# Normalising row tile 0 on GpSimd, and summing half of the layernorm scale on VectorE

## The chip, the cores and the metric

The kernel runs on one core of one Trainium2 chip. The metric is the device time of one execution in microseconds. Most executions of the kernel before agree within 0.3%; each comparison below is made with runs of the kernel before on the same chip in the same rounds. All runs compared here are of the state "fast". Kernels of different rounds ran partly on different chips and are set side by side by their medians (the kernel before had 831.05 to 831.30 us there).

Engine names in the profile: PE is TensorE (products), PEld its weight loads, DVE is VectorE, ACT is ScalarE, POOL is GpSimd, SP is the engine whose queue issues the DMAs.

## The reference

One transformer block with adaptive layernorm: linear attention, then a gated feed-forward part. Only the first layernorm and the first product matter here.

```python
mod = (silu(c) @ w_mod).reshape(c.shape[0], 6, 1, -1)      # c: 1 x 1024, w_mod: 1024 x 6144
sa, ca, ga, sb, cb, gb = (mod[:, i] for i in range(6))
h = layernorm(x) * (1 + ca) + sa                           # x: 2048 x 1024
x = x + ga * linear_attention(h, wqkv, wo)                 # starts with h @ wqkv
...                                                        # feed-forward part: not touched
```

`sa` is the shift and `ca` the scale of the first layernorm. Each is a vector of 1024, the product of `silu(c)` with a 1024 x 1024 block of `w_mod`.

## The kernel before

A helper records every operation with what it reads and writes, and sets the semaphores from that; so every instruction carries the same source line, L176, and is told apart by its tiles. PSUM dependencies are kept by whole banks.

The first chunk of 512 rows has four row tiles of 128. They are normalised (`XRES`), transposed on TensorE, scaled, and used as the moving operand of the q products (a k-tile is 128 of the 1024 values over which these products sum). The scale comes from 64 one-column products per 1024 columns (8 column tiles x 8 k-tiles), into single columns of PSUM bank 0:

```python
def ln1_xn(st):                                    # normalise row tile st on VectorE
    P.dve("tensor_scalar", out=XRES[:, st, :], in0=XRES[:, st, :],
          scalar1=MV[:, st, 0:1], scalar2=RSTD[:, st:st + 1], op0=ALU.subtract, op1=ALU.mult)

def mod_sc(w, c0, ms):                             # scale or shift, column tiles ms, on TensorE
    for m in ms:
        for kt in range(NDT):
            P.pe("matmul", out=PS[:, 0, c0 + m:c0 + m + 1], lhsT=w[:, kt, m * 128:(m + 1) * 128],
                 rhs=SILUC[:, kt:kt + 1], start=mod_first[0], stop=(kt == NDT - 1), skip_group_check=True)
            mod_first[0] = False
```

The start and the first q products (`q_part` is one 128x128 by 128x512 product for each k-tile given):

```python
ca_load(0); wq_load(0, 2); ca_load(1); wq_load(2, 2); wq_load(4, 2); sa_load(1)   # ca_load: 512 columns
...
ln1_xn(0); tile_transposes(0)
ln1_xn_act(1); tile_transposes(1)                  # tile 1 is normalised on ScalarE
...
ln1_xn(2); ln1_xn(3)
mod_sc(WCA, 8, range(2)); fin_ca(0, 2)             # scale columns 0-255, then + 1 into MODCOL
tile_transposes(2, 3)
h0_first(0, "dve"); h0_first(1, "dve")             # scale k-tiles 0, 1
...
for nt in range(4):
    q_part(nt, qb[nt], (0,))
mod_sc(WCA, 8, range(2, 4)); fin_ca(2, 2)          # columns 256-511
... 10 more q products ...
mod_sc(WCA, 8, range(4, 8)); fin_ca(4, 4)          # columns 512-1023: 32 one-column products
for dt in (4, 5):
    h0_scale_only(dt)
for nt in range(7):
    q_part(nt, qb[nt], (2, 3))
act_stats(4)
for nt in range(7):
    if nt == 4:
        mod_sc(WSA, 0, range(6, 8)); fin_sa(6, 2)  # shift
        for dt in (6, 7):
            h0_scale(dt)
    q_part(nt, qb[nt], (4, 5))
...
```

Of the kernel before, what the change touches and what calls it, by code (L numbers as in the profile page):

```python
# [6 lines left out]
BF16 = mybir.dt.bfloat16  # L7
U8 = mybir.dt.uint8
ACT = mybir.ActivationFunctionType
# [253 lines left out]
def bass_adaLN_cond__linear_attn_block__swiglu_ffn__prompt_kernel(  # L263
# [22 lines left out]
    with ExitStack() as es:  # L286
# [6 lines left out]
        def T(name, off, shape, dt):  # L293
            n = 1
            for s_ in shape[1:]:
                n *= s_
            assert off % 32 == 0 and off + n * mybir.dt.size(dt) <= ARENA, (name, off, shape)
            return nc.alloc_sbuf_tensor_at(name, shape, dt, offset=base + off)
# [29 lines left out]
        ZCOL = T("zcol", SM + 2304, [128, NHG], FP32)  # L328
        RED = T("red", SM + 2336, [128, NDT], FP32)
        MASK4 = T("mask4", SM + 2368, [128, 4], BF16)  # L330
        BIASQ = T("biasq", SM + 2784, [128, NDT], FP32)
        SUMXH = T("sumxh", SM + 2816, [128, NST, 2], FP32)
        NMR = T("nmr", SM + 2944, [128, NST], FP32)
# [64 lines left out]
        for st in range(4):  # L398
            P.dma("x0_%d" % st, XRES[:, st, :], xv[:, st, :])

        def ca_load(p):
            P.dma("wca%d" % p, WCA[:, :, 512 * p:512 * p + 512], wmv[:, :, D + 512 * p:D + 512 * p + 512])

        def sa_load(p):
            P.dma("wsa%d" % p, WSA[:, :, 512 * p:512 * p + 512], wmv[:, :, 512 * p:512 * p + 512])
# [1 line left out]
        def wq_load(i, n=1):  # L407
            P.dma("wq%d" % i, WQK[:, i:i + n, 0:D], wqkvv[:, i:i + n, 0:D])

        ca_load(0)  # L410
        wq_load(0, 2)
        ca_load(1)
        wq_load(2, 2)
        wq_load(4, 2)
        sa_load(1)
# [27 lines left out]
        P.dve("memset", ap=MASK[:], constant=0.0)  # L443
        for h in range(4):
            P.dve("memset", ap=MASK[32 * h:32 * h + 32, 32 * h:32 * h + 32], constant=1.0)
        P.dve("memset", ap=MASK4[:], constant=0.0)
        for h in range(4):
            P.dve("memset", ap=MASK4[32 * h:32 * h + 32, h:h + 1], constant=1.0)
# [4 lines left out]
        def warm(n=1, bank=2):  # L453
            for _ in range(n):
                P.pe("matmul", out=PS[:, bank, :], lhsT=IDENT[:], rhs=E1[:, 0, :], start=True, stop=True)
# [61 lines left out]
                P.dve("tensor_copy", out=MODTMP[:, m:m + n], in_=PS[:, 0, m:m + n])  # L517
            P.dve("tensor_copy", out=MODCOL[:, 1, m:m + n], in_=PS[:, 0, m:m + n])

        def h0_scale_only(dt):  # L520
            P.dve("tensor_scalar", out=HT[:, 0, dt, :], in0=HT[:, 1, dt, :], scalar1=MODCOL[:, 0, dt:dt + 1],
                  scalar2=None, op0=ALU.mult)

# [27 lines left out]
            else:  # L551
                P.dve("tensor_copy", out=dst, in_=src)

        def h0_scale(dt):
            P.dve("tensor_scalar", out=HT[:, 0, dt, :], in0=HT[:, 1, dt, :], scalar1=MODCOL[:, 0, dt:dt + 1],
                  scalar2=MODCOL[:, 1, dt:dt + 1], op0=ALU.mult, op1=ALU.add)

# [16 lines left out]
        def act_stats(st, c0=0, mid=None):  # L574
            n = (D - c0) // 512
            junk0 = HT[:, 1, 0:2, :] if st < 8 else JUNK1
            for fn_, sc_, acc_ in ((ACT.Identity, 1.0 / D, SUMX), (ACT.Square, D ** -0.5, SUMSQ)):
                P.act("activation", out=junk0[:, 0:n, :], in_=XRES[:, st, c0:D].rearrange("p (a b) -> p a b", a=n),
                      func=fn_, scale=sc_, accum_out=acc_[:, st:st + 1])
                if mid is not None:  # L580
                    mid()
                    mid = None

        def act_mv_ops(st):
            return [
                lambda: P.dve("tensor_copy", out=MV[:, st, 0:1], in_=SUMX[:, st:st + 1]),
                lambda: P.dve("scalar_tensor_tensor", out=MV[:, st, 1:2], in0=SUMX[:, st:st + 1],
                              scalar=SUMX[:, st:st + 1], in1=SUMSQ[:, st:st + 1], op0=ALU.mult, op1=ALU.subtract),
            ]
# [3 lines left out]
                  op1=ALU.add)  # L593
            P.pool("tensor_tensor", out=RSTD[:, st:st + 1], in0=VE[:, st:st + 1], in1=NEGHALF[:, 0:1], op=ALU.pow)

        act_stats(2)
        s0_, s1_, s3_ = ln1_stats_ops(0), ln1_stats_ops(1), ln1_stats_ops(3)
        m2 = act_mv_ops(2)

        def tile_transposes(*js):  # L600
            for dt in range(NDT):
# [3 lines left out]
                         identity=IDENT[:])  # L605

        warm(13, bank=3)
        s0_[0]()
        s0_[1]()
        s1_[0]()  # L610
        s0_[2]()
        ln1_rstd1(0)
        s1_[1]()
        s1_[2]()
        ln1_rstd1(1)
        ln1_xn(0)
        tile_transposes(0)
        warm(5, bank=3)
        s3_[0]()
        ln1_xn_act(1)  # L620
        tile_transposes(1)
        warm(0, bank=3)
        m2[1]()
        m2[0]()
        neg_rstd(2)
        s3_[1]()
        s3_[2]()
        ln1_rstd1(3)
        ln1_xn(2)
        ln1_xn(3)  # L630
        mod_sc(WCA, 8, range(2))
        fin_ca(0, 2)
        tile_transposes(2, 3)
        h0_first(0, "dve")
        h0_first(1, "dve")
        raw_copy(4, "dve")
# [95 lines left out]

        def q_phase_chunk0(side):
            qb = [1, 2, 3, 4, 6, 7, 5]
            for nt in range(4):
                q_part(nt, qb[nt], (0,))
            mod_sc(WCA, 8, range(2, 4))
            fin_ca(2, 2)
            for dt in (2, 3):
                h0_first(dt, "dve")  # L740
            for nts, dts in (((4, 5), (0,)), (range(6), (1,)), ((6,), (0, 1))):
                for nt in nts:
                    q_part(nt, qb[nt], dts)
            mod_sc(WCA, 8, range(4, 8))
            fin_ca(4, 4)
            for dt in (4, 5):
                h0_scale_only(dt)
            for nt in range(7):
                q_part(nt, qb[nt], (2, 3))
            act_stats(4)  # L750
            for nt in range(7):
                if nt == 4:
                    mod_sc(WSA, 0, range(6, 8))
                    fin_sa(6, 2)
                    for dt in (6, 7):
                        h0_scale(dt)
                q_part(nt, qb[nt], (4, 5))
            mod_sc(WSA, 0, range(4, 6))
            fin_sa(4, 2, True)
# [437 lines left out]
```

## Time and profile before

| | before |
|---|---|
| time, median of 3 (range) | 831.13 us (830.97 to 832.21) |
| share of the chain of waits on TensorE | 98% |
| first q product | 12.29 us |
| TensorE idle after that | under 0.1 us at any place |
| two scalings of k-tiles 0 and 1 (VectorE) before it | 0.88 us |

The page's part on the chain that ended last, by engine, for the kernel before:

```profile
PE 98%; DMA 1%; DVE 0%; ACT 0%; SPq 0%; POOL 0%; issue 0%
```

The same chain in order of time; the columns are start in us, length in us, and what the chain stood on:

```profile
9.78 0.79 POOL rstd L176
...
10.60 0.56 DVE xres L176
...
11.20 1.01 PE ps L176 x15
...
12.29 814.80 PE ps L176 x4016
```

The chain goes through the last reciprocal root on GpSimd, the normalisation of the last tile on VectorE and 15 transposes; then it is TensorE without a break to the end. Whatever the first q product waits for sets the time one for one; after it, so does every product added or taken away and every wait of TensorE.

The timeline of the kernel before on TensorE; columns are start, length, engine, line, operation, tiles written and read, shapes, count, and in brackets the idle before it with what ended it:

```profile
12.29 1.02 PE L176 MATMUL ps<-ht,wqk 128*128 128x512 bf16 x4
13.15 0.54 PE L176 MATMUL ps<-siluc,wca 128*128 128x1 bf16 x16
13.56 2.32 PE L176 MATMUL ps<-ht,wqk 128*128 128x512 bf16 x10
15.71 0.94 PE L176 MATMUL ps<-siluc,wca 128*128 128x1 bf16 x32
16.51 4.91 PE L176 MATMUL ps<-ht,wqk 128*128 128x512 bf16 x22
```

From starts alone: 32 one-column products occupy 16.51 - 15.71 = 0.80 us, so 0.025 us each, and 10 q products 15.71 - 13.56 = 2.15 us, so 0.215 us each. (A product's own length, 0.38 us, overlaps the next and is of no use here.)

Two more groups matter for estimating what the change adds. First the running sum that the kernel already makes later for other rows of `w_mod` (count, then shortest, median and longest in ns, first and last start, shape):

```profile
L176 DVE SCALAR_TENSOR_TENSOR acc<-stg,siluf,acc x14: 1275/1278/1286, 84.3 to 125.6; 128x1024 f32<-128x1024 bf16 x14
...
L176 DVE TENSOR_TENSOR mhl<-acc,mhl x4: 1224/1226/1226, 99.6 to 279.2; 128x1024 bf16<-128x1024 f32 x4
```

And the scaling that GpSimd does in it:

```profile
L176 POOL TENSOR_SCALAR h2t<-h2t,modcol x32: 762/768/1180, 230.9 to 649.4; 128x512 bf16<-128x512 bf16 x32
```

### The profile page before, as it was taken

The page shows a single profiled execution, that of the slowest core. Times are in us where ns is not written, and L with a number is a line of the kernel's source. Part 1 is how long each engine was busy: PE and PEld are TensorE (multiplying, and loading weights), DVE is VectorE, ACT ScalarE, POOL GpSimd, SP SyncE. Part 2 cuts the span into 40 slices and gives each one's busy share as a digit, 9 for nine tenths or more (in the row PEclk, how much of TensorE's full clock was granted, in tenths as well). Part 3 has the DMA queues.
Part 4 walks back from the last instruction along what each step waited for, and adds up shares of the span by engine and source line. Part 5 has one row for each costly group of instructions (what it writes and reads, how often), then busy time and mean ns, then how long its engine had stood idle before and what let it go on. Part 6 is the DMA issues. An engine that isn't in the chain of part 4 may idle for free.

```text
span 829.3 us, 10017 instructions
## 1 busy us (share of the span) xinstructions
PE 823.3 (99%) x4083; PEld 378.8 (46%) x4083; DVE 312.9 (38%) x666; ACT 196.3 (24%) x335; POOL 40.5 (5%) x58
## 2 busy tenths in 40 slices
PE   8999999999999999999999999999999999999998
PEld 4544444454444444444444444444444444444444
DVE  5797986756955521121221111122111211221111
ACT  3658641323232111111111111111110111111011
POOL 1010000000130000030000003000000300000000
DMA  9969655938297986700455571045557004553000
GB/s 320 284 152 229 150 162 172 197 107 304 57 256 226 262 256 184 194 25 13 123 152 153 152 188 34 13 124 154 152 153 193 27 13 124 151 154 91 0 26 26
DMA packets 199246, 119.29 MB, mean 144 GB/s; under 512 B 57880, under 2 KB 182944, under 8 KB 199200
## 3 DMA queue, kind: packets, MB, share of 16 engines
q1 hardware_dynamic: 199184, 118.65, 53.0%
q8 instruction: 32, 0.52, 0.3%
q14 instruction: 14, 0.11, 0.0%
q10 hardware_dynamic: 16, 0.00, 0.0%
HBM read 100.67 MB, written 4.33 MB: 127 GB/s over the span
## 4 chain that ended last, share of the span: by engine, by line
PE 98%; DMA 1%; DVE 0%; ACT 0%; SPq 0%; POOL 0%; issue 0%
PE ps L176 98%; DMA xres<-in_A_x_dram 1%; ACT ht L176 0%; DVE xres L176 0%; SPq L176 0%; POOL rstd L176 0%; DVE stats L176 0%; DVE mv L176 0%; DVE ve L176 0%
## 5 line engine op out<-in xcount | busy, mean ns | idle before, releaser
L176 PE MATMUL ps<-h2t,gug 128*128 128x512 bf16 x896 | 211.7, 379 | 0.0
L176 PE MATMUL ps<-h2t,guu 128*128 128x512 bf16 x896 | 211.7, 379 | 0.0
L176 DVE TENSOR_TENSOR at<-sg,ps 128x512 bf16<-128x512 bf16 x112 | 77.0, 687 | 282.8 <-PE ps L176 281.2
L176 ACT ACTIVATE sg<-ps 128x512 bf16<-128x512 f32 x112 | 66.9, 597 | 309.7 <-PE ps L176 309.7
L176 PEld LDWEIGHTS ps<-h2t,guu 128*128 128x128 bf16 x896 | 87.7, 98 | 105.7
L176 PEld LDWEIGHTS ps<-h2t,gug 128*128 128x128 bf16 x896 | 87.6, 98 | 105.5
L176 PE MATMUL ps<-wd_a,at 128*128 128x512 bf16 (+1 forms) x512 | 112.4, 377 | 0.0
L176 PE MATMUL ps<-ht,wqk 128*128 128x512 bf16 x512 | 111.8, 379 | 0.1
L176 PE MATMUL ps<-wd_b,at 128*128 128x512 bf16 (+1 forms) x384 | 85.0, 377 | 0.0
L176 PEld LDWEIGHTS ps<-wd_a,at 128*128 128x128 bf16 x512 | 50.1, 98 | 59.7
L176 DVE TENSOR_TENSOR ut<-att,gb_b 128x512 bf16<-128x512 bf16 (+1 forms) x32 | 14.1, 441 | 167.0 <-ACT att L176 167.0
L176 PEld LDWEIGHTS ps<-ht,wqk 128*128 128x128 bf16 x512 | 49.4, 98 | 58.7 <-issue 0.2
L176 ACT ACTIVATE att<-ps 128x512 bf16<-128x512 f32 (+1 forms) x32 | 17.4, 591 | 182.1 <-PE ps L176 182.1
L176 PEld LDWEIGHTS ps<-wd_b,at 128*128 128x128 bf16 x384 | 37.6, 98 | 44.7
L176 PE MATMUL ps<-pk,xres 128*128 128x512 bf16 x256 | 56.5, 379 | 0.0
L176 PE MATMUL ps<-mw,pqt 128*128 128x512 bf16 x256 | 56.3, 379 | 0.0
L176 POOL TENSOR_SCALAR h2t<-h2t,modcol 128x512 bf16<-128x512 bf16 x32 | 26.3, 836 | 383.4 <-DMA h2t<-xn 383.4
L176 ACT ACTIVATE e<-ps 128x512 bf16<-128x512 f32 x56 | 33.1, 603 | 31.8 <-PE ps L176 21.3
L176 PEld LDWEIGHTS ps<-mw,pqt 128*128 128x128 bf16 x256 | 24.8, 98 | 30.2 <-DVE xres L176 0.4
L176 PEld LDWEIGHTS ps<-pk,xres 128*128 128x128 bf16 x256 | 24.8, 98 | 30.0 <-issue 0.4
L176 ACT ACTIVATE junk<-xres 128x1024 bf16<-128x1024 bf16 x24 | 25.4, 1058 | 35.1 <-DVE xres L176 34.9
L176 DVE SCALAR_TENSOR_TENSOR xres<-ps,xres 128x512 bf16<-128x512 f32 x32 | 21.4, 688 | 12.3 <-PE ps L176 11.5
(106 smaller groups left out, 345.1 us busy)
## 6 DMA issues: line engine op xcount, KB each, us to landing
gug<-in_B_w_gate_dram SPq DMA_DIRECT2D x56, 512.0 KB, 3.9
guu<-in_B_w_up_dram SPq DMA_DIRECT2D x56, 512.0 KB, 5.2
xres<-in_A_x_dram SPq DMA_DIRECT2D x20, 256.0 KB, 8.0
rb<-recip_den SPq DMA_DIRECT2D x8, 512.0 KB, 11.5
stgx<-in_w_mod_dram SPq DMA_DIRECT2D x2, 2048.0 KB, 7.8
wd_a<-in_B_w_down_dram SPq DMA_DIRECT2D x4, 1024.0 KB, 8.0
out_dram<-xres SPq DMA_DIRECT2D x31, 128.0 KB, 1.7
xres<-in_A_x_dram SPq DMA_DIRECT2D x3, 1024.0 KB, 14.2
```

Source lines behind the costliest of these rows:

```text
L176: return getattr(e, method)(**kw)
```

## The change

Intent: take work off TensorE in the q phase and off VectorE at the start. Scale columns 512-1023 are accumulated over the 8 k-tiles on VectorE in fp32, split into a bf16 high and low part, and summed over partitions by 2 one-column products for each column tile (8 products instead of 32). Columns 256-511 move ahead of the first q product. Tile 0 is normalised on GpSimd; tile 1 is transposed after tile 2. The scale columns come in four loads of 256 columns instead of two of 512. Two scalings move to ScalarE. The diff is cut: not shown are the new order of the first statistics and of the q products, tile 2's normalisation straight from its sums, the earlier place of the products for columns 0-255, and fewer filler products.

```diff
-        def ca_load(p):
-            P.dma("wca%d" % p, WCA[:, :, 512 * p:512 * p + 512], wmv[:, :, D + 512 * p:D + 512 * p + 512])
+        def ca_load(c0, c1):
+            P.dma("wca%d" % c0, WCA[:, :, c0:c1], wmv[:, :, D + c0:D + c1])
...
-        ca_load(0)
+        ca_load(0, 256)
+        ca_load(256, 512)
         wq_load(0, 2)
-        ca_load(1)
+        ca_load(512, 768)
+        ca_load(768, 1024)
         wq_load(2, 2)
...
+        def part_macc(w, c0, c1):
+            for kt in range(NDT):
+                if kt == 0:
+                    P.dve("tensor_scalar", out=ACC[:, c0:c1], in0=w[:, kt, c0:c1], scalar1=SILUF[:, kt:kt + 1],
+                          scalar2=None, op0=ALU.mult)
+                else:
+                    P.dve("scalar_tensor_tensor", out=ACC[:, c0:c1], in0=w[:, kt, c0:c1], scalar=SILUF[:, kt:kt + 1],
+                          in1=ACC[:, c0:c1], op0=ALU.mult, op1=ALU.add)
+            P.dve("tensor_copy", out=MHL[:, 0, c0:c1], in_=ACC[:, c0:c1])
+            P.dve("tensor_tensor", out=MHL[:, 1, c0:c1], in0=ACC[:, c0:c1], in1=MHL[:, 0, c0:c1], op=ALU.subtract)
+
+        def part_sum(c0, ms):
+            for m in ms:
+                for i in range(2):
+                    P.pe("matmul", out=PS[:, 0, c0 + m:c0 + m + 1], lhsT=MHL[:, i, m * 128:(m + 1) * 128],
+                         rhs=ONESC[:], start=False, stop=(i == 1), skip_group_check=True)
...
+        def xn_pool(st):
+            P.pool("tensor_scalar", out=XRES[:, st, :], in0=XRES[:, st, :],
+                   scalar1=MV[:, st, 0:1], scalar2=RSTD[:, st:st + 1], op0=ALU.subtract, op1=ALU.mult)
...
+        xn_pool(0)
         ln1_rstd1(1)
-        ln1_xn(0)
+        s3_[0]()
         tile_transposes(0)
...
+        tile_transposes(2)
+        tile_transposes(1)
         ln1_xn(3)
-        mod_sc(WCA, 8, range(2))
-        fin_ca(0, 2)
-        tile_transposes(2, 3)
+        tile_transposes(3)
+        mod_sc(WCA, 8, range(2, 4))
         h0_first(0, "dve")
         h0_first(1, "dve")
...
-            mod_sc(WCA, 8, range(4, 8))
-            fin_ca(4, 4)
-            for dt in (4, 5):
-                h0_scale_only(dt)
+            part_macc(WCA, 512, 768)
             for nt in range(7):
+                if nt == 3:
+                    part_sum(8, (4, 5))
+                    fin_ca(4, 2)
+                    h0_scale_only(4)
+                    h0_scale_only(5, "act")
+                    part_macc(WCA, 768, 1024)
                 q_part(nt, qb[nt], (2, 3))
-            act_stats(4)
             for nt in range(7):
                 if nt == 4:
+                    part_sum(8, (6, 7))
+                    fin_ca(6, 2)
                     mod_sc(WSA, 0, range(6, 8))
                     fin_sa(6, 2)
-                    for dt in (6, 7):
-                        h0_scale(dt)
+                    h0_scale(6)
+                    h0_scale(7, "act")
+                    act_stats(4)
                 q_part(nt, qb[nt], (4, 5))
```

More of the change, by code (lines that the diff above doesn't have):

```diff
@@ L330, in bass_adaLN_cond__linear_attn_block__swiglu_ffn__prompt_kernel @@
         MASK4 = T("mask4", SM + 2368, [128, 4], BF16)
+        ONESC = T("onesc", SM + 2400, [128, 1], BF16)
         BIASQ = T("biasq", SM + 2784, [128, NDT], FP32)
@@ L445, in bass_adaLN_cond__linear_attn_block__swiglu_ffn__prompt_kernel @@
             P.dve("memset", ap=MASK[32 * h:32 * h + 32, 32 * h:32 * h + 32], constant=1.0)
+        P.dve("memset", ap=ONESC[:], constant=1.0)
         P.dve("memset", ap=MASK4[:], constant=0.0)
@@ L518, in fin_sa, with h0_scale_only @@
             P.dve("tensor_copy", out=MODCOL[:, 1, m:m + n], in_=PS[:, 0, m:m + n])
-        def h0_scale_only(dt):
+        def part_macc(w, c0, c1):
[13 more added lines that the diff above has]
+                         rhs=ONESC[:], start=False, stop=(i == 1), skip_group_check=True)
+        def h0_scale_only(dt, eng="dve"):
+            if eng == "act":
+                P.act("activation", out=HT[:, 0, dt, :], in_=HT[:, 1, dt, :], func=ACT.Copy,
+                      scale=MODCOL[:, 0, dt:dt + 1])
+                return
             P.dve("tensor_scalar", out=HT[:, 0, dt, :], in0=HT[:, 1, dt, :], scalar1=MODCOL[:, 0, dt:dt + 1],
@@ L552, in raw_copy, with h0_scale @@
                 P.dve("tensor_copy", out=dst, in_=src)
-        def h0_scale(dt):
+        def h0_scale(dt, eng="dve"):
+            if eng == "act":
+                P.act("activation", out=HT[:, 0, dt, :], in_=HT[:, 1, dt, :], func=ACT.Identity,
+                      scale=MODCOL[:, 0, dt:dt + 1], bias=MODCOL[:, 1, dt:dt + 1])
+                return
             P.dve("tensor_scalar", out=HT[:, 0, dt, :], in0=HT[:, 1, dt, :], scalar1=MODCOL[:, 0, dt:dt + 1],
@@ L594, in neg_rstd, with act_var, xn_sums @@
             P.pool("tensor_tensor", out=RSTD[:, st:st + 1], in0=VE[:, st:st + 1], in1=NEGHALF[:, 0:1], op=ALU.pow)
-        act_stats(2)
         s0_, s1_, s3_ = ln1_stats_ops(0), ln1_stats_ops(1), ln1_stats_ops(3)
-        m2 = act_mv_ops(2)
+        def act_var(st):
+            P.dve("scalar_tensor_tensor", out=MV[:, st, 1:2], in0=SUMX[:, st:st + 1], scalar=SUMX[:, st:st + 1],
+                  in1=SUMSQ[:, st:st + 1], op0=ALU.mult, op1=ALU.subtract)
+            neg_rstd(st)
+        def xn_sums(st):
+            P.dve("tensor_scalar", out=XRES[:, st, :], in0=XRES[:, st, :],
+                  scalar1=SUMX[:, st:st + 1], scalar2=RSTD[:, st:st + 1], op0=ALU.subtract, op1=ALU.mult)
+        def xn_pool(st):
+            P.pool("tensor_scalar", out=XRES[:, st, :], in0=XRES[:, st, :],
+                   scalar1=MV[:, st, 0:1], scalar2=RSTD[:, st:st + 1], op0=ALU.subtract, op1=ALU.mult)
         def tile_transposes(*js):
@@ L607, in bass_adaLN_cond__linear_attn_block__swiglu_ffn__prompt_kernel @@
         warm(13, bank=3)
+        act_stats(2)
         s0_[0]()
         s0_[1]()
-        s1_[0]()
         s0_[2]()
         ln1_rstd1(0)
+        s1_[0]()
         s1_[1]()
         s1_[2]()
+        xn_pool(0)
         ln1_rstd1(1)
-        ln1_xn(0)
+        s3_[0]()
         tile_transposes(0)
-        warm(5, bank=3)
-        s3_[0]()
+        warm(3, bank=3)
+        mod_sc(WCA, 8, range(2))
+        s3_[1]()
         ln1_xn_act(1)
-        tile_transposes(1)
-        warm(0, bank=3)
-        m2[1]()
-        m2[0]()
-        neg_rstd(2)
-        s3_[1]()
+        act_var(2)
         s3_[2]()
         ln1_rstd1(3)
-        ln1_xn(2)
+        xn_sums(2)
+        fin_ca(0, 2)
+        warm(1, bank=3)
+        tile_transposes(2)
+        tile_transposes(1)
         ln1_xn(3)
-        mod_sc(WCA, 8, range(2))
-        fin_ca(0, 2)
-        tile_transposes(2, 3)
+        tile_transposes(3)
+        mod_sc(WCA, 8, range(2, 4))
         h0_first(0, "dve")
@@ L734, in q_phase_chunk0 @@
             qb = [1, 2, 3, 4, 6, 7, 5]
-            for nt in range(4):
-                q_part(nt, qb[nt], (0,))
-            mod_sc(WCA, 8, range(2, 4))
             fin_ca(2, 2)
@@ L740, in q_phase_chunk0 @@
                 h0_first(dt, "dve")
-            for nts, dts in (((4, 5), (0,)), (range(6), (1,)), ((6,), (0, 1))):
+            for nts, dts in ((range(4), (0,)), (range(4), (1,)), ((4, 5, 6), (0, 1))):
                 for nt in nts:
                     q_part(nt, qb[nt], dts)
-            mod_sc(WCA, 8, range(4, 8))
-            fin_ca(4, 4)
-            for dt in (4, 5):
-                h0_scale_only(dt)
+            part_macc(WCA, 512, 768)
             for nt in range(7):
+                if nt == 3:
[4 more added lines that the diff above has]
+                    part_macc(WCA, 768, 1024)
                 q_part(nt, qb[nt], (2, 3))
-            act_stats(4)
             for nt in range(7):
                 if nt == 4:
+                    part_sum(8, (6, 7))
+                    fin_ca(6, 2)
                     mod_sc(WSA, 0, range(6, 8))
                     fin_sa(6, 2)
-                    for dt in (6, 7):
-                        h0_scale(dt)
+                    h0_scale(6)
+                    h0_scale(7, "act")
+                    act_stats(4)
                 q_part(nt, qb[nt], (4, 5))
```

## The prediction

> **What bounds the kernel.** TensorE. The chain of waits gives it 98% of the span; from 12.29 us to 827 us the chain is one unbroken piece of products (814.80 us). In the timeline 512-column products start 0.216 us apart and one-column products 0.025 us apart (32 in 0.80 us, 15.71 to 16.51)[...]. So each nanosecond of products removed after the first q product counts, and each wait put there counts in full. Only the first 30 us change.
>
> **Removed.** In the q phase the 32 one-column products for columns 512-1023 become 8: 24 x 0.025 = 0.6 us. The 16 products for columns 256-511 move ahead of the first q product, under the wait for VectorE's first scaling: 0.4 us. In all 1.0 us.
>
> **Start.** Tile 0 on GpSimd: the trace's 128x512 scalings there took 0.77 us, so about 1.5 us for 1024 columns (estimate), instead of 0.54 on VectorE; tile 1 is transposed after tile 2. The last chain (sums of tile 2, root, tile 3) loses about 0.4 us of VectorE work ahead of it. I expect the first q product near 12.0 us instead of 12.29: 0.3 us gained.
>
> **Added, and on the critical path.** The trace's accumulate step on 128x1024 fp32 took 1.28 us on VectorE, two dependent ones 2.60 us; on a 128x1 operand the same operation took 0.21 us. So 256 columns cost about [...]0.48 us, 0.52 with the gap (estimate). [...]the trace's hi/lo subtraction took 1.226[...]. One pass: 0.38 (first multiply) + 7 x 0.52 + 0.33 (cast) + 0.46 = about 4.75 us.
> - Pass 1 can start about 1.8 us after the first q product, ending at 6.6. TensorE reaches the partition sum after 20 q products = 4.3 us. It waits about 2.3 us.
> - Then 16 q products (3.45 us) are available, but before pass 2 ends VectorE needs the bank read, one scaling and another pass, about 5.7 us. Wait about 2.1 us.
> - After the second sum, the shift products write the same PSUM bank that the scale's read holds: a round trip TensorE-VectorE-TensorE, about 0.45 us.
>
> **DMA.** Columns in 512-byte pieces: the trace's gate/up loads with that form went at about 300 GB/s against about 355 for 1 KB rows, so 2 MB takes 1 us more. Weights for k-tiles 2-3 land near 16.4 instead of 15.34 us, after TensorE wants them; that wait is hidden in the first 2.3 us.
>
> **Sum.** -1.0 - 0.3 + 2.3 + 2.1 + 0.45 = about +3.7. Time: 834.9 us, range 833.0 to 836.4. Faster by over 2%: 0.3%; within 2%: 99%; slower by over 2%: 0.7%.
>
> **Profile.** Right: accumulate steps of 0.48 us; TensorE idle twice before q products, each about 2 us, released by VectorE's hi/lo tile; a third idle of 0.4 us before the shift products; start near 12.0. Wrong: accumulate steps of 0.35 us (waits near 0.4 us, the change even), or idle released by a DMA.
>
> **What would make it wrong.** A smaller fixed cost of short VectorE operations; VectorE and GpSimd disturbing each other; a lower clock after 2 us of idling.

The sum stays as it came to, about +3.7 us, and none of its terms is cut; but its two waits, 2.3 and 2.1 us, rest on the pass of 4.75 us, and in that pass the 0.46 us rests on the cut 0.42. The trace of before supports about the same values: the accumulate step's 1.28 us on 1024 columns and 0.21 on one give 0.48 on 256 by a straight line (estimate), and the hi/lo subtraction's 1.226 us on 1024 and 0.169 on 8 give 0.43 (estimate). The 0.38 and 0.33 us for the first multiply and the cast are estimates; in the trace they took 0.75 and 0.68 us on 1024 columns.

## The result, and the profile after

The change took 838.89 us (median of 6, 837.55 to 840.36) against 831.17 us (median of 6): a ratio of 1.0093, 95% interval 1.0079 to 1.0106. The change is slower by 7.7 us, not by 3.7; within 2%, but well outside the predicted range.

| | before | after |
|---|---|---|
| first q product | 12.29 us | near 15.9 us |
| from it to the end of the last bias products (shift times q weights; end of the q phase's extra work) | 15.5 us | 20.4 us |
| rest of the kernel, to the last product | 799.0 us | 799.7 us |
| granted TensorE clock, profiled run | 1.0 | 0.994 |

(The profiled run of after is one of the two slowest of the six; a fiftieth of the product records is missing from its trace, the first q product among them.) Nearly all of the loss lies in the first 36 us: 8.5 of the 9.1 us by which these two spans differ.

The chain of the kernel after, by engine; the page also has a row for the granted clock now, which before had not:

```profile
PE 88%; DVE 6%; DMA 3%; issue 1%; POOL 1%; SPq 0%; ACT 0%; DVEq 0%; ACTq 0%; POOLq 0%
```

Tile 0 before, on VectorE:

```profile
6.64 0.54 DVE L176 TENSOR_SCALAR xres<-xres,mv,rstd 128x1024 bf16<-128x1024 bf16 x1
```

The timeline of the kernel after, all engines, cut to the lines that set the pace:

```profile
6.12 3.79 POOL L176 TENSOR_SCALAR xres<-xres,mv,rstd 128x1024 bf16<-128x1024 bf16 x1
...
9.96 1.03 PE L176 MATMUL ps<-ident,xres 128*128 128x128 bf16 x8 [2.72 <-POOL xres L176]
...
12.92 2.77 PE L176 MATMUL ps<-ident,xres 128*128 128x128 bf16 x24
...
16.28 4.26 PE L176 MATMUL ps<-ht,wqk 128*128 128x512 bf16 x19 [0.19 <-issue]
...
17.91 3.61 DVE L176 SCALAR_TENSOR_TENSOR acc<-wca,siluf,acc 128x256 f32<-128x256 bf16 x7
...
21.90 0.18 PE L176 MATMUL ps<-onesc,mhl 128*128 128x1 bf16 x1 [1.36 <-DVE mhl L176]
...
22.36 0.23 PE L176 MATMUL ps<-onesc,mhl 128*128 128x1 bf16 x3 [0.28 <-DVE mhl L176]
...
27.47 0.18 PE L176 MATMUL ps<-onesc,mhl 128*128 128x1 bf16 x1 [1.40 <-DVE mhl L176]
...
27.93 0.23 PE L176 MATMUL ps<-onesc,mhl 128*128 128x1 bf16 x3 [0.28 <-DVE mhl L176]
...
28.51 0.54 PE L176 MATMUL ps<-siluc,wsa 128*128 128x1 bf16 x16 [0.35 <-DVE modcol L176]
```

Read it from the top. GpSimd took 3.79 us for tile 0, and TensorE sat idle for it. GpSimd is also the engine of the reciprocal roots, so the root of tile 1 (9.87 us) queued behind. Then 24 transposes took 2.77 us where 15 took 1.01 before: they ran at the half clock (0.50) shown below; at full clock, in tile0_on_vector, 24 took 1.51 us. Later TensorE waited twice for VectorE's hi/lo tile, each time 1.4 us, then 0.28 us more between the first hi and the first lo product, and once for the read of the scale. The brackets understate a wait, since a product's modelled end lies after its slot (a q product has 0.38 us of length in a slot of 0.215): by start to start, less the product's own slot, the gaps are 1.52 + 0.44, 1.57 + 0.44 and 0.49 us.

The windows view of the kernel after; the number after the brackets is the granted clock, then the DMA share and GB/s:

```profile
5.90:9.40 3.50, 1.34 (x6) 0.39 (x4) 2.24 (x5) 2.30 (x4) 3.40 (x2) 1.00 1.10 317
9.40:16.20 6.80, 6.13 (x68) 4.99 (x70) 2.96 (x11) 1.72 (x2) 2.22 (x4) 0.50 1.12 333
16.20:29.80 13.60, 9.76 (x63) 4.48 (x64) 11.37 (x29) 3.28 (x5) 0.00 (x0) 1.00 1.08 361
29.80:33.30 3.50, 3.50 (x40) 1.79 (x39) 0.23 (x2) 2.48 (x5) 0.00 (x0) 0.51 1.09 357
```

The same view for the 3.41 us around the first wait for a sum and around the second:

```profile
19.63:23.04 3.41, 1.77 (x12) 0.67 (x10) 2.88 (x8) 0.22 (x1) 0.00 (x0) 1.00 1.08 364
26.46:29.87 3.41, 1.69 (x24) 1.15 (x26) 2.04 (x7) 0.59 (x1) 0.00 (x0) 1.00 1.09 360
```

The first pair of numbers is TensorE's busy time: 1.34 of 3.5 us in the first stretch, and in the next 6.8 us the clock is half (0.50). After the second wait for a sum it is half again for 3.4 us (0.51). The half-clock stretches are 6.83 us and 3.41 us long and begin 20.48 us apart, six times 3.41. Ahead of them TensorE was not idle throughout: it was busy for 1.34 of 3.5 us before the first and for 1.69 of 3.41 us before the second, while 1.77 of 3.41 us, around the first wait for a sum, was not followed by a half clock.

The accumulate steps themselves were as predicted, 0.48 us on 256 columns:

```profile
L176 DVE SCALAR_TENSOR_TENSOR acc<-wca,siluf,acc x14: 484/485/485, 17.9 to 26.6; 128x256 f32<-128x256 bf16 x14
```

So the waits for the sums were foreseen in kind and size; the GpSimd operation (2.5 times its estimate) and the half clock were not in the sum. What is open at this point: why GpSimd needed 3.79 us; how much of the start is the wait and how much the clock; and whether the loads, whose wait could be hidden behind the others, cost anything.

### The profile page after: what moved, and what is told of

Its sections match the earlier page's. It is cut to its first block, busy times and chain, and to the rows that moved or that the text cites. A ratio compares the mean times of both kernels' runs of the same rounds, so it can differ in the third digit from the quotient of the medians.

```text
span 838.4 us, 9915 instructions
## 1 busy us (share of the span) xinstructions
PE 822.6 (98%) x3981; PEld 380.5 (45%) x4058; DVE 320.7 (38%) x684; ACT 197.6 (24%) x337; POOL 44.2 (5%) x59
## 4 chain that ended last, share of the span: by engine, by line
PE 88%; DVE 6%; DMA 3%; issue 1%; POOL 1%; SPq 0%; ACT 0%; DVEq 0%; ACTq 0%; POOLq 0%
PE ps L176 88%; DVE acc L176 3%; DMA stg<-in_w_mod_dram 1%; DMA z_row<-zr 1%; DMA mhlt<-mhl 1%; DVE mhl L176 1%; DVE pkt L176 1%; DVE e L176 0%; POOL xres L176 0%; DMA zb<-z_row 0%; DVE ht L176 0%; DMA xres<-in_A_x_dram 0%; DVE pqt L176 0%; SPq L176 0%; DVE red L176 0%
```

## The experiments

Fourteen further kernels ran on the chip besides the one that measured GpSimd alone, fifteen in all. All gave correct results. Times are medians of 5 runs with the range (idle_filled: 4 runs; the one with the GpSimd forms: one run).

| kernel | us (range) | ratio to before, 95% interval |
|---|---|---|
| the change | 838.89 (837.55 to 840.36) | 1.0093 (1.0079 to 1.0106) |
| gpsimd_alone_forms | 836.80 (one run, state unknown) | not compared |
| tile0_on_vector | 836.87 (836.30 to 837.87) | 1.0070 (1.0057 to 1.0083) |
| sums_on_tensor | 834.28 (833.43 to 835.17) | 1.0038 (1.0025 to 1.0050) |
| both_undone | 833.54 (832.88 to 834.66) | 1.0028 (1.0014 to 1.0042) |
| gpsimd_add_form | 836.80 (836.36 to 837.39) | 1.0069 (1.0056 to 1.0081) |
| idle_filled | 838.34 (838.15 to 838.83) | 1.0087 (1.0073 to 1.0101) |
| both_undone_wide_loads | 831.99 (831.24 to 832.16) | 1.0008 (0.9995 to 1.0020) |
| tensor_only_reordered | 830.85 (830.79 to 831.28) | 0.9998 (0.9984 to 1.0012) |
| sums_only | 836.46 (835.39 to 836.81) | 1.0060 (1.0048 to 1.0073) |
| gpsimd_only | 834.30 (833.05 to 835.34) | 1.0042 (1.0029 to 1.0056) |
| start_reordered | 830.88 (830.83 to 831.57) | 0.9999 (0.9986 to 1.0011) |
| start_reordered_quarter_sum | 833.32 (832.70 to 835.07) | 1.0032 (1.0019 to 1.0044) |
| four_loads_1kb | 831.55 (831.08 to 832.30) | 1.0007 (0.9995 to 1.0020) |
| sums_only_filled | 836.25 (835.64 to 836.53) | 1.0060 (1.0048 to 1.0073) |
| change_wide_loads | 837.82 (836.95 to 839.92) | 1.0080 (1.0067 to 1.0094) |

### tile0_on_vector

```diff
-        xn_pool(0)
+        ln1_xn(0)
         ln1_rstd1(1)
```

> The change with one line undone: tile 0 is normalised on VectorE again. Theory A (the GpSimd scaling, 3.79 us in the trace of after where the prediction had 1.5, holds back the second root and so everything up to the first q product, and the idle it leaves also halves the granted TensorE clock from 9.4 to 16.2 us): the first q product comes back from 15.9 to near 12.0 us, and the time to 834.4 us, or to 836 if the waits for the sums alone still bring one stretch of half clock. Rival B (the late start comes from the new order of the operations or from the 512-byte loads): the first q product stays later than 14 us and the time above 837.

Measured: the first q product came at 11.94 us and the time was 836.87 us. Rival B falls for the start: neither the order nor the loads delay it. But only 2.0 us came back, not the 4 us by which the start moved. Its timeline on TensorE shows a wait in a place where after had none:

```profile
11.94 3.18 PE L176 MATMUL ps<-ht,wqk 128*128 128x512 bf16 x14
...
16.71 1.47 PE L176 MATMUL ps<-ht,wqk 128*128 128x512 bf16 x6 [1.59 <-DMA wqk<-in_A_wqkv_dram]
18.07 0.18 PE L176 MATMUL ps<-onesc,mhl 128*128 128x1 bf16 x1
18.53 0.23 PE L176 MATMUL ps<-onesc,mhl 128*128 128x1 bf16 x3 [0.28 <-DVE mhl L176]
```

With the start early, TensorE waits 1.59 us for the weights of k-tiles 2-3, and in that time VectorE finishes the first sum: the first wait for the sum has changed its name. Two causes lay over one another, and taking one away uncovered the other. This alone does not account for what did not come back: the q phase, to the end of the last bias products, is as long as in after (20.5 and 20.4 us). The spans of the two profiled runs differ by 2.7 us: 3.9 gained at the start and 1.1 lost in a later stage, from the first product on `pk` to the first on `mw` (62.22 us against 61.08 in after and 60.83 before), where TensorE waits once for VectorE:

```profile
152.30 4.06 PE L176 MATMUL ps<-pk,xres 128*128 128x512 bf16 x18 [1.23 <-DVE g L176]
```

This stage "near 150 us" comes back below.

### sums_on_tensor

```diff
-            part_macc(WCA, 512, 768)
...
-                    part_sum(8, (4, 5))
+                    mod_sc(WCA, 8, range(4, 6))
...
-                    part_macc(WCA, 768, 1024)
...
-                    part_sum(8, (6, 7))
+                    mod_sc(WCA, 8, range(6, 8))
```

> The change with the sums undone: columns 512-767 and 768-1023 are 16 one-column products each on TensorE, at the places in the q phase where the partition sums stood; GpSimd keeps tile 0. If the two waits of about 2 us each for the hi/lo tile are what the sums cost, the start stays near 15.9 us, the waits of 1.5 + 0.4 us go, the second stretch of half clock (29.9 to 33.3 us) goes with them, and the time is near 834.9 us. If the waits are only moved (TensorE then waits for a weight load or a column load instead), it stays above 837.

Measured: 834.28 us, as the first reading had it. The waits for the hi/lo tile are gone. The start in its profile was 14.97 us (15.9 had been expected), with one stretch of half clock (9.7 to 13.1 us) instead of two.

### both_undone

The two edits above together.

> Both undone: what remains of the change is the order of the tiles, the four column loads of 256 columns, two scalings on ScalarE, and the 16 products moved ahead of the first q product. If only the start and the sums cost, and the 512-byte pieces do not matter: 830.9 us (start near 12.0 us, 0.4 us of products hidden, 0.5 us lost on the round trip before the shift products). If the weights of k-tiles 2-3, which landed at 16.9 us in after against 15.3 before, are now waited for (q products of k-tile 2 are due 3.0 us after the first q product): 832.8 us, with an idle of TensorE of about 1.5 to 1.9 us near 15 us released by a DMA.

Measured: 833.54 us, and in the profile the wait that the second reading named, though 0.7 us more was lost than it said (0.45 us of it, in the profile, in the stage near 150 us, 61.28 us):

```profile
17.26 1.47 PE L176 MATMUL ps<-ht,wqk 128*128 128x512 bf16 x6 [1.45 <-DMA wqk<-in_A_wqkv_dram]
```

The weights of k-tiles 2-3 landed at 17.2 us, against 15.3 before. So a third part of the change has a cost, which the other two hid. The first q product here was at 12.63 us; from run to run the first loads of x land some 0.5 us apart (tile 3 at 6.2 to 7.7 us in the profiles), and the start tends to move with them (11.94 us where tile 3 landed at 6.7, 12.63 where it landed at 7.4).

### gpsimd_alone_forms

The kernel with tile 0 on VectorE and, in a quiet stretch of the feed-forward part, on a scratch tile:

```diff
+                if ch == 1 and ft == 4:
+                    P.pool("memset", ap=PROBE[:], constant=0.5)
+                    for n in (1024, 512):
+                        for a0, a1 in ((ALU.subtract, ALU.mult), (ALU.mult, ALU.add), (ALU.add, ALU.mult)):
+                            for _ in range(2):
+                                P.pool("tensor_scalar", out=PROBE[:, 0:n], in0=PROBE[:, 0:n], scalar1=MV[:, 0, 0:1],
+                                       scalar2=RSTD[:, 0:1], op0=a0, op1=a1)
```

> The kernel with tile 0 on VectorE, plus twelve GpSimd scalings of a scratch tile in the second chunk of the feed-forward part, where VectorE and the DMA queues are lightly used: 1024 columns, then 512, each as subtract-multiply, multiply-add and add-multiply, twice each. If 3.79 us was contention at the start (bn statistics on VectorE, loads at 350 GB/s), subtract-multiply of 1024 takes about 1.5 us here[...]. If it is the form of the operation, subtract-multiply takes about 3.8 us at 1024 and 1.9 at 512 here too, and multiply-add 1.5 and 0.77. If it is the length, all three forms take 3.8 at 1024 and 0.77 at 512.

The timeline of GpSimd there; in order two subtract-multiply, two multiply-add and two add-multiply of 1024 columns, then the same of 512 (the last of the 1024s and the last three left out):

```profile
366.74 3.79 POOL L176 TENSOR_SCALAR probe<-probe,mv,rstd 128x1024 bf16<-128x1024 bf16 x1
370.62 3.78 POOL L176 TENSOR_SCALAR probe<-probe,mv,rstd 128x1024 bf16<-128x1024 bf16 x1
374.50 1.71 POOL L176 TENSOR_SCALAR probe<-probe,mv,rstd 128x1024 bf16<-128x1024 bf16 x1
376.31 1.24 POOL L176 TENSOR_SCALAR probe<-probe,mv,rstd 128x1024 bf16<-128x1024 bf16 x1
377.65 1.20 POOL L176 TENSOR_SCALAR probe<-probe,mv,rstd 128x1024 bf16<-128x1024 bf16 x1
...
380.24 2.08 POOL L176 TENSOR_SCALAR probe<-probe,mv,rstd 128x512 bf16<-128x512 bf16 x1
382.42 2.07 POOL L176 TENSOR_SCALAR probe<-probe,mv,rstd 128x512 bf16<-128x512 bf16 x1
384.59 0.77 POOL L176 TENSOR_SCALAR probe<-probe,mv,rstd 128x512 bf16<-128x512 bf16 x1
```

VectorE beside the first multiply-add:

```profile
375.26 1.22 DVE L176 TENSOR_TENSOR xres<-xres,ut 128x512 bf16<-128x512 bf16 x1
```

It is the form of the operation. Subtract-then-multiply takes 3.79 us on 1024 columns with VectorE idle and no DMA traffic to speak of beside it (19 GB/s from 352 to 394 us in the trace of before, where this stretch lies), just as at the start beside loads at 317 GB/s, and 2.07 on 512. Multiply-then-add and add-then-multiply take 1.19 to 1.24 us on 1024, and multiply-then-add 0.77 on 512. Contention plays no part in the 3.79 us. It is not absent elsewhere: the first multiply-add, with VectorE at work beside it, took 1.71 us, the two add-multiplies of 512 columns 0.84 and 1.06, and VectorE's addition at 375.26 took 1.22 us, where such additions with nothing on GpSimd beside them take 0.42 to 0.43 in this trace. Why the subtract form is slow was not looked into. The spacing from start to start agrees with the spans: 370.62 - 366.74 = 3.88 us for a span of 3.79, 382.42 - 380.24 = 2.18 for 2.08.

### gpsimd_add_form

```diff
         def xn_pool(st):
+            P.dve("tensor_scalar", out=NMR[:, st:st + 1], in0=MV[:, st, 0:1], scalar1=-1.0, scalar2=None, op0=ALU.mult)
             P.pool("tensor_scalar", out=XRES[:, st, :], in0=XRES[:, st, :],
-                   scalar1=MV[:, st, 0:1], scalar2=RSTD[:, st:st + 1], op0=ALU.subtract, op1=ALU.mult)
+                   scalar1=NMR[:, st:st + 1], scalar2=RSTD[:, st:st + 1], op0=ALU.add, op1=ALU.mult)
```

> The change with the GpSimd scaling written as add (of the negated mean, one more tiny VectorE operation) and multiply; the values are the same. By the scratch-tile runs this form takes 1.2 to 1.3 us on 1024 columns where subtract-multiply takes 3.79. Theory A (only the slow form of the GpSimd operation makes the late start): the scaling takes about 1.3 us, the first q product comes near 12.2 us instead of 15.9, and the time equals that of the kernel with tile 0 on VectorE, 836.9 us, within 0.6. Rival (GpSimd work at the start is held up by, or holds up, VectorE and the loads whatever its form): the scaling stays over 2 us and the time over 838.

Measured: 836.80 us, equal to tile 0 on VectorE (836.87), in other rounds. In its profile the first q product came at 12.52 us, after

```profile
7.04 1.19 POOL L176 TENSOR_SCALAR xres<-xres,nmr,rstd 128x1024 bf16<-128x1024 bf16 x1 [0.92 <-DVE ve L176]
```

So moving tile 0 to GpSimd is not harmful in itself; its slow form was. It is not a gain over VectorE either.

### idle_filled

Products of zeros in the three long waits of the change (`MASKZ` is a tile of zeros; the output columns are unused):

```diff
+        warm(12, bank=3)
         tile_transposes(0)
...
+        def fill(n):
+            for _ in range(n):
+                P.pe("matmul", out=PS[:, 0, 64:512], lhsT=IDENT[:], rhs=MASKZ[:], start=False, stop=True,
+                     skip_group_check=True)
+
         def part_sum(c0, ms):
+            fill(7)
```

> The change as it is, with products of zeros put into TensorE's three long waits: 12 before the transposes of tile 0 (2.6 us) and 7 of 448 columns into unused columns of bank 0 before each partition sum (1.3 us). The waits themselves cannot shrink. Theory: on top of the waits, about 3.3 us of the loss is half clock after them (9.4 to 16.2 us and 29.9 to 33.3 us in the trace of after). Then the clock is 1.0 throughout, the first q product comes near 14.4 us instead of 15.9, the products after the second sum run at 0.216 us, and the time is near 835.6 us with less scatter between runs (838.9, 837.6 to 840.4 in after). Rival (the half clock costs nothing beside the waits): 838.9 or a little more.

Measured: the clock stayed at 1.0 in all four runs, the first q product came at 14.61 us in the profile, and the scatter shrank from 2.8 us to 0.7. But the median fell by 0.5 us only, to 838.34. In its profile a wait of 1.4 us stood near 152 us which in after was 0.25: some of what was gained was lost there again (more on it below). Beside the profile of after, the start is about 1.2 us earlier, the q phase about 1.2 us shorter (19.3 against 20.4) and the stage near 150 us 1.1 us longer (62.20 against 61.08). The theory is right about the clock and the start; its size in the total did not come out, and by the median (835.6 expected, 838.9 by the rival) the rival is not refuted.

### both_undone_wide_loads

```diff
-        ca_load(0, 256)
-        ca_load(256, 512)
+        ca_load(0, 512)
         wq_load(0, 2)
-        ca_load(512, 768)
-        ca_load(768, 1024)
+        ca_load(512, 1024)
         wq_load(2, 2)
```

> The kernel with both undone (833.5 us), with the two column loads of 512 columns, in 1 KB pieces, of the kernel before. There TensorE waited 1.45 us near 16 us for the weights of k-tiles 2-3. If the 512-byte pieces make these late, they land near 15.4 us instead of 16.9 or more, the wait shrinks to about 0.3 us and the time is near 832.2. If they are late for another reason (order of issue, queue), the wait and 833.5 stay.

Measured: 831.99 us, 1.5 less than with narrow loads, as expected. The weights landed at 15.7 us, and 20 q products run with 0.15 us lost between them:

```profile
12.56 4.63 PE L176 MATMUL ps<-ht,wqk 128*128 128x512 bf16 x20
```

### tensor_only_reordered

Both undone and wide loads, with the weights of k-tiles 2-3 issued ahead of columns 512-1023, and the shift products ahead of the scale's read:

```diff
-        ca_load(512, 1024)
         wq_load(2, 2)
+        ca_load(512, 1024)
...
-                    fin_ca(6, 2)
                     mod_sc(WSA, 0, range(6, 8))
+                    fin_ca(6, 2)
                     fin_sa(6, 2)
```

> A version meant to be faster: both undone, wide loads, the weights of k-tiles 2-3 loaded ahead of columns 512-1023, and the shift products issued ahead of the read of the scales, so that no round trip lies between them. If the account of the parts is right, what is left of the change is a start 0.3 us earlier and 0.4 us of products hidden under it: 830.6 us, no wait of TensorE over 0.3 us after the first q product. If the new tile order itself costs something that the other terms hid: 831.3 or more.

Measured: 830.85 us, a ratio of 0.9998: the same as before. Removing the round trip worked (no gap before the shift products), and from the first q product to the end of the last bias products it took 27.58 - 12.43 = 15.15 us against 27.84 - 12.29 = 15.55 before, the 0.4 us of products that had been moved. But the first q product was at 12.43 us, not 12.0, so little was left in the total.

### sums_only

The wide-loads kernel, and the sums as in the change (tile 0 on VectorE).

> The kernel with both undone and wide loads (832.0 us) plus the VectorE sums and partition sums alone: tile 0 on VectorE, 1 KB loads. It measures the sums by themselves, without the loads that hid their first wait. Theory: TensorE waits about 1.9 us before each of the two partition sums, hand-over between the hi and the lo product included, and 24 products of 25 ns are saved: 832.0 + 3.8 - 0.6 = 835.2 us, up to 836.9 if a stretch of half clock follows the second wait. Rival (the sums' waits were mostly another thing's, the weights of k-tiles 2-3): the first wait is under 1 us and the time under 834.3.

Measured: 836.46 us, so the sums alone cost 4.5 us, at the upper end of the range. (Each of the two ratios has an interval of 1.1 us either way, so the difference is known to about 1.5 us.) With the weights in time, the first wait is the sum's:

```profile
18.52 0.18 PE L176 MATMUL ps<-onesc,mhl 128*128 128x1 bf16 x1 [1.54 <-DVE mhl L176]
...
24.09 0.18 PE L176 MATMUL ps<-onesc,mhl 128*128 128x1 bf16 x1 [1.40 <-DVE mhl L176]
```

All five runs had a clock of 0.998, which is one stretch of half clock (25.1 to 28.5 us in the profile). The rival falls.

### gpsimd_only

The wide-loads kernel, and tile 0 on GpSimd in the subtract-multiply form.

> The same base (832.0 us) plus the GpSimd scaling of tile 0 alone, in its subtract-multiply form. Theory: it ends near 9.9 us, the second root and with it tiles 1 to 3 follow, the first q product comes at 14.4 to 15.0 us instead of 12.6, and the time is about 834.1 us (a little more where a stretch of half clock falls on the transposes). Rival (the start has slack, as the difference of only 0.7 us between the kernels with and without GpSimd, both on 512-byte loads, would suggest): under 833.

Measured: 834.30 us, 2.3 more than its base, as expected (known to about 1.5 us, as above). In its profile TensorE waited for GpSimd:

```profile
9.88 0.62 PE L176 MATMUL ps<-ident,xres 128*128 128x128 bf16 x8 [1.75 <-POOL xres L176]
```

The five runs differ by how often the clock was halved, and that sorts them. Spans in us, with the mean granted clock, here and in the other kernels whose runs differ in it:

| kernel | clock 1.0 | 0.998 | 0.996 | 0.994 |
|---|---|---|---|---|
| gpsimd_only | 831.3 | 832.1, 832.6 | 833.4, 833.6 | |
| sums_on_tensor | 831.7 | 832.5, 832.5, 833.0, 833.4 | | |
| gpsimd_add_form | 834.6, 834.9, 835.0 | 835.5, 835.6 | | |
| tile0_on_vector | 834.5 | 835.0, 835.1, 835.7, 836.1 | | |
| start_reordered_quarter_sum | 831.0, 831.1, 831.6 | 833.1, 833.3 | | |
| the change | 836.3 | 835.8, 836.6 | 837.7, 838.6 | 838.4 |
| change_wide_loads | | 835.2, 835.9, 836.1 | 837.1 | 838.2 |

Each step of 0.002 is one stretch of 3.4 us at half clock (0.002 x 832 = 1.7 us of clock). Within the first four kernels a step goes with 0.7 to 1.2 us more, in the fifth with 2.0; in the change itself the one run at 1.0 is no shorter than those at 0.998. That the two go together does not show that the clock is the cause: a longer wait may lie behind both, which could not be checked, since one run of each kernel has a trace. By its one run at 1.0, about 1.1 of gpsimd_only's 2.3 us is the wait itself (831.3 against a median span of 830.2 for the base) and the rest goes with the clock; this was not tested.

Whether a given run gets the stretch was not under control here, but the profiles show what goes ahead of one. Seven of them have half-clock stretches in the first 36 us, nine in all. Counted in steps of 3.41 us from these, TensorE was busy for 36 to 50.5% of the step just before each stretch, and for 50.9% or more of every other step at full clock from 4 us on (in after, 37% and 49% before its two stretches, and 52% around the first wait for a sum, which none followed). So, in these traces, a wait of 2 us gets its stretch or not by how it falls across the steps.

### start_reordered

In tensor_only_reordered, the first 16 scale products go after the transposes of tile 2:

```diff
-        mod_sc(WCA, 8, range(2))
...
         tile_transposes(2)
+        mod_sc(WCA, 8, range(2))
         tile_transposes(1)
         ln1_xn(3)
+        fin_ca(0, 2)
         tile_transposes(3)
```

> The reordered TensorE-only version (830.85 us), in which TensorE still sat idle 1.36 us near 9 us for the first columns of the scale weights, ahead of the transposes of tile 2. Here these 16 products come after the transposes of tile 2. If that wait set the start, the first q product comes near 12.0 us instead of 12.43 and the time is 830.4 us. If tile 3's normalisation sets it, nothing changes: 830.85.

Measured: 830.88 us; nothing changed. So the wait for the first scale columns was not all that set the start; that tile 3's normalisation did, as the second reading has it, is not shown by this.

### start_reordered_quarter_sum

```diff
+            part_macc(WCA, 768, 1024)
             for nt in range(7):
                 if nt == 3:
                     mod_sc(WCA, 8, range(4, 6))
                     fin_ca(4, 2)
                     h0_scale_only(4)
...
-                    mod_sc(WCA, 8, range(6, 8))
+                    part_sum(8, (6, 7))
```

> The same, with columns 768-1023 alone summed on VectorE and over partitions by four one-column products. VectorE can begin when these columns have landed (about 15.3 us) and needs 4.7 us; TensorE reaches the partition sum about 8.2 us after the first q product, near 20.2 us. If the sums cost only what TensorE waits for them, there is no wait over 0.3 us here, the hand-over between hi and lo (0.45 us) may remain, 12 products of 25 ns are saved, and the time is within 0.3 us of the version without it.

Measured: 833.32 us, 2.4 us worse than without it; the expectation failed. (The profiled run is one of the two at clock 0.998, 834.9 and 835.1 us, with a half-clock stretch from 22.8 to 26.3 us; the three at 1.0 took 832.7 to 833.3.) The partition sum was indeed not waited for. But I had put the sum into VectorE's queue ahead of two small operations that TensorE needed first. VectorE's timeline:

```profile
16.59 3.61 DVE L176 SCALAR_TENSOR_TENSOR acc<-wca,siluf,acc 128x256 f32<-128x256 bf16 x7
20.23 0.29 DVE L176 CAST mhl<-acc 128x256 bf16<-128x256 f32 x1
20.55 0.43 DVE L176 TENSOR_TENSOR mhl<-acc,mhl 128x256 bf16<-128x256 f32 x1
20.90 0.15 DVE L176 TENSOR_SCALAR modcol<-ps 128x2 f32<-128x2 f32 x1
21.09 0.35 DVE L176 TENSOR_SCALAR ht<-ht,modcol 128x512 bf16<-128x512 bf16 x1
```

The read of the scale and the scaling of k-tile 4, both due near 18 us, ran only after the sum, and TensorE's timeline has, at that end:

```profile
21.59 1.67 PE L176 MATMUL ps<-ht,wqk 128*128 128x512 bf16 x6 [1.97 <-DVE ht L176]
```

So the wait moved from the sum's consumer to whatever stood behind the sum in VectorE's queue. Whether half the sum in a better place in the queue would cost nothing was not tried.

### four_loads_1kb

both_undone, with four loads of 512 columns by four k-tiles:

```diff
+        def ca_half(c0, c1, k0):
+            P.dma("wca%d_%d" % (c0, k0), WCA[:, k0:k0 + 4, c0:c1], wmv[:, k0:k0 + 4, D + c0:D + c1])
...
-        ca_load(0, 256)
-        ca_load(256, 512)
+        ca_half(0, 512, 0)
+        ca_half(0, 512, 4)
```

(and likewise for columns 512-1023)

> The kernel with both undone, its scale columns in four loads as in the change, but each of 512 columns and four k-tiles, so in 1 KB pieces. If the 512-byte pieces cost the 1.5 us between the kernels with four narrow and two wide loads (833.5 and 832.0), the weights of k-tiles 2-3 land near 15.4 us, no wait appears near 150 us and the time is 832.0. If the number of loads does it, the weights may land in time, but the wait near 150 us (0.4 us and more) stays, with the transposing transfer before it taking 1.9 instead of 1.3 us to issue, and the time is 832.4 or more.

Measured: 831.55 us, so it is the pieces and not the count. In the profiles, a load of 512 KB landed 1.46 and 1.48 us after the one ahead of it with 1 KB pieces, and 1.58 to 1.79 us with 512-byte pieces (after and both_undone). The transposing transfer did take 1.92 us to issue with four loads of either kind (1.32 to 1.33 with two), but the stage near 150 us was only 0.2 us longer.

### sums_only_filled

sums_only with `fill(7)` in both waits, as in idle_filled.

> The kernel with the sums alone (836.46 us) with seven products of zeros in each of the two waits for the partition sums. In its profile the clock was half from 25.1 to 28.5 us, after the second wait. If this half clock is a term of its own, the clock stays at 1.0, the time falls to about 835.2 us and the scatter (835.4 to 836.8) narrows. If it costs nothing beside the wait: 836.4.

Measured: 836.25 us. The clock was 1.0 in all five runs and 0.998 in all five of sums_only, yet the spans are the same (833.9 to 834.8 against 833.6 to 835.1). Filling the waits keeps the clock up and gains nothing that these runs can resolve. Its profile had a late start (12.93 us, the first scale columns landed at 10.35 instead of near 9.7), which I can't tie to the edit. In the profiles the q phase itself, from the first q product to the end of the last bias products, did shrink: 19.4 us against near 20.7 in sums_only, where the base has 15.85. There about 3.5 us of the sums' cost stay with the clock up and 1.3 go with the half clock; the late start and 0.4 us lost before 132 us hid this gain in the total.

### change_wide_loads

The change, with the two wide loads.

> The whole change with the two wide column loads of before instead of the four narrow ones. The parts measured on the wide loads add up to 832.0 + 2.3 (GpSimd) + 4.5 (sums) = 838.8 us, where the change itself took 838.9. If the loads cost what the late wait showed in after (0.25 us near 150 us) and their other wait is hidden: 838.6. If they cost as much here as where both are undone (1.5 us): 837.4.

Measured: 837.82 us, between the readings. The ranges of this kernel and of the change overlap (836.95 to 839.92, 837.55 to 840.36), and so do the intervals of their ratios. About 1 us of the change's loss is the loads' by the medians; that is not beyond doubt.

## Why the prediction was wrong, point by point

The prediction's range ended at 836.4; the time was 838.9. The direction and the larger part of the mechanism were right: the sums put two waits of about 2 us on TensorE. One term was wrong in sign; the half clock was named but not counted, and the wait near 150 us was not foreseen. (The terms of the sum as written add up to 3.55 us, not 3.7; this changes nothing below.)

- **The step that failed: "Tile 0 on GpSimd: the trace's 128x512 scalings there took 0.77 us, so about 1.5 us for 1024 columns (estimate) ... 0.3 us gained".** The 0.77 us belonged to a multiply-add; the new operation is a subtract-multiply, which takes 3.79 us at the start and 3.79 us alone in a quiet stretch. Written as add-multiply it takes 1.19 us, and the change is then as fast as with tile 0 on VectorE. The first q product came near 15.9 us instead of 12.0. Measured by itself (gpsimd_only against its base), the step cost 2.3 us instead of gaining 0.3; undone in the change it gave 2.0 back. This is 2.3 to 2.6 of the 4.0 us by which the prediction missed. The start at 12.0 us is not confirmed by any run with tile 0 on GpSimd: in the fast form, quicker than the 1.5 us assumed, it came at 12.52 us. With tile 0 on VectorE it came at 11.94 and 12.63 us (tile0_on_vector, both_undone), so a gain over 12.29 is not shown.
- **The sums: predicted 2.3 + 2.1 - 0.6 = 3.8 us, measured 4.5 us.** The accumulate steps took 0.485 us (0.48 estimated), the hi/lo subtraction 0.43. The waits with hand-over are 1.96 and 2.01 us in after, against 2.3 and 2.1. The 0.7 us above is less than the 1.5 us to which the 4.5 is known. In the q phase of the profiles the sums cost 3.5 us where the clock stayed up and 4.8 with the one stretch of half clock that every run of sums_only had.
- **The round trip before the shift products: predicted 0.45, measured 0.49 us.** tensor_only_reordered has it no more.
- **The half clock was named among what could go wrong, and put at nothing in the sum.** Within single kernels a stretch of it goes with 0.7 to 2.0 us; after's runs had between none and three (clock 1.0 to 0.994). Its share in the medians was not isolated: the two kernels that kept the clock at 1.0 with products of zeros gained 0.5 and 0.2 us, though the q phases of their profiles were 1.2 and 1.3 us shorter.
- **The loads: predicted 1 us later, "hidden in the first 2.3 us".** The weights did land later, 16.9 instead of 15.3 us in after, and TensorE did not wait for them there. Where the other two parts are undone the narrow loads cost 1.5 us; in the change, 1.1 by medians whose ranges overlap.

The parts, each measured on wide loads, add up: 831.99 (order and the rest) + 2.3 (GpSimd) + 4.5 (sums) = 838.8, against 837.8 measured for the two together and 838.9 with narrow loads. They are additive to about 1 us, no better, because the waits overlap: with narrow loads, GpSimd costs 834.28 - 833.54 = 0.7 us only, since the late start covers the late weights.

What stays open: the wait near 150 us, which in the profiles took 1.1 us back from tile0_on_vector and from idle_filled. There TensorE waits for VectorE, VectorE for ScalarE (3.5 us at most in after) and ScalarE for a row that comes back by DMA (16.7 us in after). The stage it belongs to (from the first product on `pk` to the first on `mw`) was 0.25 to 1.4 us longer than before's 60.83 us in every profiled kernel with 256-column loads, 0.2 us with four 1 KB loads, and at most 0.1 us with two wide ones. Why loads at 10 us reach so far was not found.

No version here beats the kernel before: the best two, at 0.9998 and 0.9999, are the same.

## What to carry to other kernels

Estimate an operation from a trace only with a group of the same operations as well as the same engine and type; on GpSimd, subtract-multiply cost three times add-multiply here (3.79 against 1.19 us on 1024 columns), so write a subtraction of a per-partition value there as an addition of its negative. When TensorE bounds a kernel, work taken off it must be finished by the time TensorE reaches its consumer: 24 products of 25 ns were bought with two waits of 2 us, and whatever stands behind the new work in the other engine's queue waits as well (TensorE lost 1.97 us to that in start_reordered_quarter_sum). Undo parts both singly and together, since a wait for one thing can hide a later one for another.
